# Inverse softmax sums as nine rows or by products, weights summed on TensorE, and a new order of work

## The chip, the cores and the metric

The kernel runs on one core of a Trainium2 chip. The engines of the core work side by side: TensorE (PE, with its weight loads as PEld), VectorE (DVE), ScalarE (ACT), GpSimd (POOL), and SyncE (SP), which issues the DMAs here. Each runs its own instructions in order and waits for the others by semaphores. The metric is the device time of one execution in microseconds. Before the change its median is 1305.22 us over three runs (1303.49 to 1308.19).

## The reference

Attention with a top-32 mask over 8 batches x 8 heads x 576 tokens x 64, then a feed-forward block over the 4608 tokens, all in float32 results:

```python
scores = scale * np.matmul(q, k.transpose(0, 1, 3, 2))
kth = np.partition(scores, -top_k, axis=-1)[..., -top_k:-top_k + 1]
scores = np.where(scores >= kth, scores, -1000000000.0)
scores = scores - np.max(scores, axis=-1, keepdims=True)
attn = np.exp(scores)
attn = attn / (np.sum(attn, axis=-1, keepdims=True) + 1e-09)
attn_out = np.matmul(attn, v)
...
h = x @ w_in                      # x: (4608, 512), w_in: (512, 1024)
e = np.exp(h - h_max)
solu = h * (e / (np.sum(e, axis=-1, keepdims=True) + 1e-09))
ln = (solu - mu) / np.sqrt(var + 1e-06) * g_ln
out = ln @ w_out                  # w_out: (1024, 512)
```

q, k, v arrive as float32. The weights arrive as 64-bit floats (4 MB each), so the kernel has to make float32 out of pairs of 32-bit words itself.

## The kernel before

**Tiling.** The attention part runs in 32 steps, four for each batch. A step takes four chunks of 128 queries (two pairs of heads, two chunks each) and one tile of left-over queries (64 of each of two heads): nine tiles of 128 x 576 scores, which the code numbers j = 0 to 8. Per tile PE makes scores (s_ps, L1951), ACT brings them to SBUF (X, L1960), and ACT and DVE find the 32nd largest score of each row: a first count of entries above an estimated threshold (L1968 on DVE, L1976 on ACT), a second one by signs (sg, L2025), the entries nearest to the threshold (w, L2046), their best eight per half (L2057), and a few merges of small rows (by, L2074 and on). `keep` (L2127, DVE) multiplies the exponentials E by the mask and sums each row into den_all. PE transposes the masked exponentials (tp_p, L2164), ACT copies them out (PT, L2177), and PE multiplies them with v (om, L2220 and L2229).

**The inverse sums.** The product om has head dimensions on its partitions and queries along its free axis, so dividing by the row sums needs the inverse sums spread over partitions. `inverse` (L2133, DVE) takes the reciprocals of 9 columns of 128 sums (rden). `rd_out` (L2138, SP) writes them to a small DRAM buffer, rows, of shape 9 x 128; as the source has queries on partitions, this is a write in 4-byte pieces. `rd_in` (L2145 and L2150, SP) reads the rows back with four DMAs, each broadcast over 64 partitions, into the tile scales (one buffer). `copy_v` (L2243 and L2250, DVE) multiplies om by scales into xTm and xTt, the input of the feed-forward part. A second half of a step has its own copy_v.

**Tokens.** The feed-forward part works on 36 token tiles of 128. `mm1` (h_ps, L2261) multiplies with w_in, `hexp` (ACT, L2272) takes exponentials, `solu` (DVE, L2280) forms the product, `square` (ACT, L2290), `spread` (POOL, L2296 and L2300) and `ln` (POOL, L2303) normalise, `transpose_ln` (PE, L2311) and `copy_ln` (ACT, L2317) turn it, `mm2` (o_ps, L2322) multiplies with w_out, `store` (ACT, L2329) and `send` (SP, L2333) bring it out. Two token tiles of a batch can start once the first two of its four steps are done, the other two after the last two, and one more tile takes the left-over queries of two batches.

**Weights.** There are 16 chunks of 128 x 512 weights, 8 of w_in and 8 of w_out. `load_w` (L1679, SP) brings a chunk of 512 KB as 64-bit words. `w_bits` (DVE, L1696, L1700, L1704) makes a truncated float32 from the high word, and from it the bare power of two. `w_low` (ACT, L1712) turns the low word into a float of at most one unit, `w_mul` (POOL, L1736) multiplies the two, `w_add` (POOL, L1739) adds this correction, and for w_out `w_gain` (POOL, L1746) multiplies by g_ln. The scratch tile w_tmp shares two buffers, the tag solu, with the token part. Near the end the weights are read a second time (w_again) and their exponents checked.

**The order of work.** The instructions of PE, ACT, DVE and POOL are not ordered by hand. `work_of` (L491) lists every operation with its engine, an estimated duration, what it comes after, and which buffers it holds (`room` gives how many there are: 2 of big, tp and o in PSUM, 1 of rb, the scales tile). `arranged` (L734) is a list scheduler over this: it takes, engine by engine, the waiting operation with the lowest rank among those that can start soon. A rank is the step's number times 36000 plus an entry of the table `PLACES` (L812 and on). The whole order is thus fixed when the program is built. SP's DMAs follow in the same order in one queue, so a DMA that waits for data holds those behind it.

At the end of the program `w_verdict` compares counts of checks; were one to fail, a slower general path would compute the output.

Of the kernel before, what the change touches and what calls it, by code (L numbers as in the profile page):

```python
# [15 lines left out]
P = 128  # L16
# [426 lines left out]
class Work:  # L443
# [18 lines left out]
    "ends", "keep", "ln", "key_stats", "w_bits", "w_mul", "w_add", "w_gain",  # L462
# [23 lines left out]

def few_of(i):
    return FEW_COUNTS[i] if i < len(FEW_COUNTS) else FEW


def work_of(B, NP, steps, NF, w_wide):  # L491
# [5 lines left out]
        "xTm": 2, "xTt": 1, "PT0": 1, "PT1": 1, "qkt": 1, "sums": 3, "st": 4, "rb": 1, "rows": 3, "w8": 2, "small": 3,  # L497
# [9 lines left out]
    for b in range(B):  # L507
        for hp in range(NP):
            n = pair(b, hp)
            add(("load_k", n), "SP", 550, behind("load_k", n), [("km", n)], late=2400)  # L510
            add(("load_t", n), "SP", 1650, behind("load_t", n), [("qkt", n)], late=2000)
            add(("load_v", n), "SP", 1650, behind("load_v", n), [("vm", n), (f"vd{n % 4}", n)], late=2400)
            add(("prep_t", n), "PE", 218, [("load_t", n)], [("qkt", n), ("o", ("pre", n)), ("kT", n)], mode="f")
            add(("prep_tc", n), "ACT", 305, [("prep_t", n)], [("o", ("pre", n)), ("kT", n)], 130)
            add(("prep_k", n), "PE", 436, [("load_k", n)], [("km", n), ("tp", ("k", n)), ("kT", n)], mode="f")
# [5 lines left out]
    for i, (b, chunks) in enumerate(steps):  # L521
# [52 lines left out]
        add(("inverse", i), "DVE", 86, [("keep", i, j) for j in range(NT)], [("small", i)], 80)  # L574
        add(("rd_out", i), "SP", 550, [("inverse", i)], [("rows", i), ("small", i)], 2200)
        add(("rd_in", i), "SP", 2200, [("rd_out", i)], [("rows", i), ("rb", i)], 2200)
# [14 lines left out]
        for part in range(2):  # L591
# [18 lines left out]
                [("attn_t", i, part), ("rd_in", i)], [("o", (i, part)), ("rb", i)] + x, 100)  # L610

    def ready_of(n):
        return ("w_gain", n) if n >= 8 else ("w_add", n) if w_wide else ("load_w", n)
# [9 lines left out]
    for m, (b, t, x, made) in enumerate(tokens):  # L623
# [3 lines left out]
        add(("hexp", m), "ACT", 1007, [("mm1", m, 0), ("mm1", m, 1)], [("big", ("h", m)), ("e", m), ("solu", m)], 115)  # L627
# [19 lines left out]
    for n in range(NW):  # L647
        if w_wide:
            tag = ("X", ("w", n)) if 2 <= n < 6 else ("E", ("w", n)) if 6 <= n < 10 else ("lnT", ("w", n))
            add(("load_w", n), "SP", 1700, behind("load_w", n), [tag], 3500)  # L650
            add(("w_bits", n), "DVE", 1600, [("load_w", n)], [tag, ("solu", ("w", n))], 80)
            add(("w_low", n), "ACT", 590, [("w_bits", n)], [tag], 100)
            add(("w_mul", n), "POOL", 1600, [("w_low", n)], [tag, ("solu", ("w", n))])
            add(("w_add", n), "POOL", 1600, [("w_mul", n)], [("solu", ("w", n))])
# [4 lines left out]
        if n >= 8:  # L659
            add(("w_gain", n), "POOL", 1080, [("w_add", n) if w_wide else ("load_w", n), ("copy_g",)])  # L660
# [69 lines left out]
WEIGHT_KINDS = ("load_g", "turn_g", "copy_g", "load_w", "w_bits", "w_low", "w_mul", "w_add", "w_gain")  # L730
# [3 lines left out]
def arranged(work, rank):  # L734
# [23 lines left out]
    while len(start) < len(ops):  # L758
# [56 lines left out]
        "K0": [-269098],  # L815
        "K1": [-754507],
        "K2": [-3281419],
        "K3": [-167927],
        "K4": [-572179],
        "K5": [-504458],  # L820
        "K6": [-165669],
        "K7": [-50556],
        "k0": [-206493],
        "k1": [-596606],
        "k2": [-1347572],
        "k3": [-1214976],
    },
    "load_t": {
        "K0": [-508282],
        "K1": [-149973],  # L830
        "K2": [254494],
        "K3": [79729],
        "K4": [-847916],
        "K5": [124341],
        "K6": [764047],
        "K7": [136089],
        "k0": [-327033],
        "k1": [-94369],
        "k2": [399104],
        "k3": [-638502],  # L840
    },
    "load_v": {
        "K0": [92658],
        "K1": [-145121],
        "K2": [-1256832],
        "K3": [105300],
        "K4": [40735],
        "K5": [-232440],
        "K6": [587722],
        "K7": [168596],  # L850
        "k0": [172383],
        "k1": [-311970],
        "k2": [-126126],
        "k3": [-893372],
    },
    "prep_t": {
        "K0": [-301887],
        "K1": [-1472896],
        "K2": [-2211926],
        "K3": [-87830],  # L860
        "K4": [-605571],
        "K5": [-1210677],
        "K6": [262025],
        "K7": [97718],
        "k0": [-70748],
        "k1": [-1446235],
        "k2": [-655124],
        "k3": [-698217],
    },
    "prep_tc": {  # L870
        "K0": [223057],
        "K1": [-863846],
        "K2": [-877564],
        "K3": [288157],
        "K4": [115939],
        "K5": [-463637],
        "K6": [634678],
        "K7": [292029],
        "k0": [50474],
        "k1": [-597275],  # L880
        "k2": [135481],
        "k3": [-95548],
    },
    "prep_k": {
        "K0": [217554],
        "K1": [423765],
        "K2": [-1151820],
        "K3": [459174],
        "K4": [138923],
        "K5": [239007],  # L890
        "K6": [314486],
        "K7": [542921],
        "k0": [212661],
        "k1": [413375],
        "k2": [429],
        "k3": [407069],
    },
    "prep_kc": {
        "K0": [22479],
        "K1": [-1263182],  # L900
        "K2": [-2452471],
        "K3": [572117],
        "K4": [-155826],
        "K5": [-931816],
        "K6": [48150],
# [1532 lines left out]
```

## Time and profile before

| | us |
|---|---|
| median of three runs | 1305.22 (1303.49 to 1308.19) |
| the profiled execution, its own time | 1310.73 |
| its span, first to last instruction | 1308.9 |
| ACT busy | 1011.4 |
| POOL busy | 209.3 |
| PE busy, mm2 (L2322) | 261.4 in 576 products |
| PE busy, mm1 (L2261) | 263.7 in 576 products |
| DVE busy, best of w (L2057) | 225.8 in 576 instructions |
| DVE busy, keep (L2127) | 236.4 in 288 instructions |
| POOL busy, w_mul and w_add | 46.1 in 32 instructions |

The mean granted TensorE clock is 0.947 of full speed. The DMA engines moved 65.45 MB in 161534 packets; 128136 of these are under 512 bytes.

How to read it: busy time counts the time in which an engine executes something; waits are not in it. In the chain of waits the profile goes back from the last instruction, at each step to what released it, or to the instruction before it on its engine. In a group's row, the idle time is that of the engine just before these instructions, with what ended most of it. In a timeline each row gives the start, the length, engine, line and operation, out<-in, the number merged into the row, and in brackets the idle time ahead of it with its releaser. In the rows of waits the three numbers are the total in us, the times, and the longest.

### The profile page before, as it was taken

How to read it: one execution, taken by the hardware profiler on the slowest of the kernel's cores; microseconds unless marked ns; L12 is line 12 of the kernel's file. 1: busy time of each engine (PE TensorE's matmuls, PEld its weight loads, DVE VectorE, ACT ScalarE, POOL GpSimd, SP SyncE). 2: the span in 40 equal slices, each digit the busy share in tenths (PEclk: the TensorE clock that was granted, in tenths of full speed). 3: DMA queues.
4: the chain of work that ended last, by engine and by line, in shares of the span. 5: the costliest groups of instructions: out<-in, count | busy, mean ns of one | idle time of the engine just before them, and what ended most of it. 6: DMA issues, size and time to landing. Idle time of an engine off the chain costs nothing.

```text
span 1308.9 us, 18612 instructions
## 1 busy us (share of the span) xinstructions
PE 1156.4 (88%) x5731; PEld 658.3 (50%) x5731; DVE 1065.6 (81%) x3065; ACT 1011.4 (77%) x2142; POOL 209.3 (16%) x207
## 2 busy tenths in 40 slices
PE   5660789888999999999999899999999999999977
PEld 3430545455555555555555455555555555555533
DVE  4869749787989889999989589999989689989811
ACT  7773677578897889889796699779796798878732
POOL 3323331010202002020203002020213002110100
PEclk8585899998999999999999899999999999999989
DMA  7231111111131112214130113213120113123630
GB/s 192 79 89 30 43 46 50 36 28 29 20 70 34 31 30 56 73 21 47 47 66 10 30 25 54 70 20 48 43 69 10 30 28 50 38 21 71 150 85 28
DMA packets 161534, 65.45 MB, mean 50 GB/s; under 512 B 128136, under 2 KB 152720, under 8 KB 161424
## 3 DMA queue, kind: packets, MB, share of 16 engines
q1 hardware_dynamic: 161424, 64.15, 22.6%
q8 instruction: 48, 0.79, 0.3%
q14 instruction: 62, 0.51, 0.2%
HBM read 54.53 MB, written 9.58 MB: 49 GB/s over the span
## 4 chain that ended last, share of the span: by engine, by line
DVE 37%; PE 35%; DMA 11%; ACT 11%; issue 3%; SPq 1%; POOL 1%; DVEq 0%; ACTq 0%; POOLq 0%
PE o_ps L2322 8%; DVE E L2127 8%; PE h_ps L2261 8%; DVE w L2046 7%; DVE w L2057 6%; PE s_ps L1951 6%; DMA rows<-rden 6%; DVE junkv L1968 6%; PE om L2220 5%; ACT sg L2025 3%; PE tp_p L2164 3%; ACT X L1960 2%; DVE solu L2280 2%; ACT E L2082 2%; PE tp_ln L2311 1%
## 5 line engine op out<-in xcount | busy, mean ns | idle before, releaser
L2322 PE MATMUL o_ps<-w_out,lnT 128*128 128x512 f32 x576 | 261.4, 599 | 0.3
L2261 PE MATMUL h_ps<-w_in,xTm 128*128 128x512 f32 x512 | 234.8, 605 | 12.7 <-DVE xTm L2243 11.4
L2057 DVE MAX8 w<-w 128x8 f32<-128x288 f32 x576 | 225.8, 445 | 0.5
L2025 ACT ACTIVATE sg<-X,t 128x576 bf16<-128x576 f32 x256 | 197.3, 781 | 29.9 <-DVE t L2010 29.4
L2127 DVE SCALAR_TENSOR_TENSOR E<-X,kth,E 128x576 f32<-128x576 f32 x256 | 210.5, 851 | 4.6 <-ACT E L2082 2.8
L1960 ACT ACTIVATE X<-s_ps 128x576 f32<-128x576 f32 x256 | 163.8, 662 | 62.3 <-PE s_ps L1951 58.2
L2046 DVE SCALAR_TENSOR_TENSOR w<-X,al,sg 128x576 f32<-128x576 f32 x256 | 206.0, 828 | 1.0
L1968 DVE TENSOR_SCALAR_CACHE_REDUCE junkv<-X,t 128x576 bf16<-128x576 f32 x216 | 174.4, 807 | 23.8 <-ACT X L1960 16.3
L2164 PE MATMUL tp_p<-ident,E 128*128 128x128 f32 x1024 | 154.5, 283 | 44.1 <-DVE E L2127 37.5
L1951 PE MATMUL s_ps<-kT,qT 64*128 64x288 f32 x1024 | 177.4, 452 | 3.3 <-ACT X L1960 2.5
L2164 PEld LDWEIGHTS tp_p<-ident,E 128*128 128x128 f32 x1024 | 117.9, 143 | 95.9 <-ACT w_raw L1712 29.1
L2322 PEld LDWEIGHTS o_ps<-w_out,lnT 128*128 128x128 f32 x576 | 106.6, 193 | 110.6 <-issue 108.7
L2177 ACT COPY PT<-tp_p 128x512 f32<-128x512 f32 x256 | 146.9, 595 | 17.4 <-PE tp_p L2164 17.0
L2220 PE MATMUL om<-PT,vm 128*64 128x256 f32 (+1 forms) x1024 | 145.5, 428 | 10.2 <-issue 6.3
L2261 PEld LDWEIGHTS h_ps<-w_in,xTm 128*128 128x128 f32 x512 | 94.4, 193 | 114.0 <-issue 95.9
L2082 ACT ACTIVATE E<-X 128x1152 f32<-128x1152 f32 x128 | 151.0, 1185 | 0.0
L1951 PEld LDWEIGHTS s_ps<-kT,qT 64*128 64x128 f32 x1024 | 99.5, 197 | 67.8 <-issue 30.2
L2296 POOL TENSOR_SCALAR var<-var 128x1 f32<-128x1 f32 x36 | 14.7, 408 | 641.2 <-ACT e_sb L2290 641.2
L1919 POOL TENSOR_TENSOR zs<-zs,phalf 128x9 f32<-128x9 f32 x32 | 61.8, 1934 | 324.2 <-DVE zs L1912 301.7
L2220 PEld LDWEIGHTS om<-PT,vm 128*64 128x64 f32 x1024 | 71.3, 142 | 68.6 <-issue 24.4
L2243 DVE TENSOR_TENSOR xTm<-om,scales 128x256 f32<-128x256 f32 x64 | 26.8, 420 | 69.5 <-DMA scales<-rows 42.8
L2272 ACT ACTIVATE e_sb<-h_ps 128x1024 f32<-128x1024 f32 x36 | 36.8, 1021 | 33.8 <-PE h_ps L2261 33.8
(132 smaller groups left out, 1515.0 us busy)
## 6 DMA issues: line engine op xcount, KB each, us to landing
km<-in_k_dram SPq DMA_DIRECT2D x32, 256.0 KB
q_sb<-in_q_dram SPq DMA_DIRECT2D x128, 64.0 KB
vm<-in_v_dram SPq DMA_DIRECT2D x32, 256.0 KB
scales<-rows SPq DMA_DIRECT2D x64, 128.0 KB
out_dram<-osb SPq DMA_DIRECT2D x32, 256.0 KB
w_raw<-in_moe_w_in_dram SPq DMA_DIRECT2D x8, 512.0 KB
w_raw<-in_moe_w_out_dram SPq DMA_DIRECT2D x8, 512.0 KB
w_again<-in_moe_w_in_dram SPq DMA_DIRECT2D x8, 512.0 KB
```

Of the source, the lines that this page charges most:

```text
L1951: nc.tensor.matmul(out=big[h][:, half, 0:SH], lhsT=queries_of(i, t)[hd, :], rhs=kT[hd, k0 : k0 + SH], start=True, stop=True,)
L1960: nc.scalar.activation(out=x_of(i, j).rearrange("p (a s) -> p a s", a=2), in_=d.pop(("s", j))[:, :, 0:SH], func=AF.Copy, scale=scale,)
L1968: nc.vector.tensor_scalar(out=junk, in0=x_of(i, j), scalar1=st[i][t][:, j : j + 1], scalar2=None, op0=ALU.is_ge, op1=ALU.add, accum_out=co ...
L2025: nc.scalar.activation(out=d["sg", j], in_=x_of(i, j), func=AF.Sign, scale=-(1.0 + 2.0**-23), bias=d["t1"][:, j : j + 1], accum_out=column ...
L2046: nc.vector.scalar_tensor_tensor(out=w, in0=x_of(i, j), scalar=d["al"][:, j : j + 1], in1=d.pop(("sg", j)), op0=ALU.subtract, op1=ALU.mult,)
L2057: nc.vector.max(w8[:, j, 8 * half : 8 * half + 8], w[:, half * SH : (half + 1) * SH])
L2082: nc.scalar.activation(out=d["E", t], in_=d["X", t], func=AF.Exp)
L2127: nc.vector.scalar_tensor_tensor(out=e, in0=x_of(i, j), scalar=d["kth"][:, j : j + 1], in1=e, op0=ALU.is_ge, op1=ALU.mult, accum_out=den_a ...
L2164: nc.tensor.transpose(tp[:, c, :], e[:, c * P : (c + 1) * P], ident)
L2220: nc.tensor.matmul(out=o[h * D : (h + 1) * D, cols], lhsT=vm[:, h, c, :], rhs=pt[:, h * NM + c, :], start=(c == 0), stop=False,)
L2261: nc.tensor.matmul(out=h[:, half, :], lhsT=x[:, c, :], rhs=w_in[:, c, half * 512 : (half + 1) * 512], start=(c == 0), stop=(c == NP - 1),)
L2322: nc.tensor.matmul(out=o, lhsT=d["lnT"][:, c, :], rhs=w_out[:, c, :], start=(c == 0), stop=(c == NF - 1),)
```

## The change

It has three parts.

**Inverse sums.** For steps 0 to 2 (`QUICK`) the DRAM trip is dropped. `spread_r` multiplies each column of inverse sums, broadcast to 64 columns as the stationary operand, with the identity on PE, so that every one of 64 output partitions holds the row; ACT copies it to scales (`copy_s`). For the other 29 steps PE turns the 128 x 9 inverse sums (`turn_r`), ACT copies the 9 x 128 result into the scales tile (`copy_r`), and the write to DRAM is nine rows of 512 bytes; the rows are put in the order head, tile, query, so that the broadcast reads are contiguous. `inverse` becomes two reciprocals for this order.

**Weights.** GpSimd has no part any more. `w_corr` on DVE makes the bare power of two and multiplies it with the low word in one instruction. `w_sum` adds the truncated float32 and the correction in PSUM by two products with the identity, the second in bf16. `w_copy` on ACT copies the sum to its place, times g_ln for w_out. The exponential of token 1 waits for the last `w_sum`.

**Order.** All entries of `PLACES`, the estimates of some DMAs, the patience of the scheduler and its price for a change of PE's mode are new; keys of one pair are prepared after those of the pair before.

```diff
+QUICK = (0, 1, 2)
...
-        add(("rd_out", i), "SP", 550, [("inverse", i)], [("rows", i), ("small", i)], 2200)
-        add(("rd_in", i), "SP", 2200, [("rd_out", i)], [("rows", i), ("rb", i)], 2200)
+        if i in QUICK:
+            for part in range(2):
+                add(("spread_r", i, part), "PE", 436 if part else 654, [("inverse", i)],
+                    [("small", i), ("tp", (i, "r", part))], mode="c")
+                add(("copy_s", i, part), "ACT", 252 if part else 360, [("spread_r", i, part)],
+                    [("tp", (i, "r", part)), ("rb", i)], 140)
+        else:
+            add(("turn_r", i), "PE", 109, [("inverse", i)], [("small", i), ("tp", (i, "r"))], mode="f")
+            add(("copy_r", i), "ACT", 157, [("turn_r", i)], [("tp", (i, "r")), ("rb", i)], 135)
+            add(("rd_out", i), "SP", 550, [("copy_r", i)], [("rows", i), ("rb", i)], 2200)
+            add(("rd_in", i), "SP", 2200, [("rd_out", i)], [("rows", i), ("rb", i)], 3000)
...
+        free = [("w_sum", 15)] if m == 1 and w_wide else []
...
-            add(("w_bits", n), "DVE", 1600, [("load_w", n)], [tag, ("solu", ("w", n))], 80)
-            add(("w_low", n), "ACT", 590, [("w_bits", n)], [tag], 100)
-            add(("w_mul", n), "POOL", 1600, [("w_low", n)], [tag, ("solu", ("w", n))])
-            add(("w_add", n), "POOL", 1600, [("w_mul", n)], [("solu", ("w", n))])
+            add(("w_bits", n), "DVE", 1160, [("load_w", n)], [tag, solu], 80)
+            add(("w_corr", n), "DVE", 1250, [("w_bits", n)], [tag, solu], 80)
+            add(("w_sum", n), "PE", 1290, [("w_corr", n)], [solu, ("tp", ("w", n))], mode="f")
+            add(("w_copy", n), "ACT", 465, [("w_sum", n)] + ([("copy_g",)] if n >= 8 else []), [("tp", ("w", n))], 135)
...
-PATIENCE = {"PE": 82, "ACT": 95, "DVE": 0, "POOL": 3677, "SP": 1016}
-TURNING = 248999
+PATIENCE = {"PE": 171, "ACT": 56, "DVE": 0, "POOL": 18243, "SP": 1014}
+TURNING = 352098
...
+    def w_corr(n):
+
+        val, corr = w_tmp[n][:, 0, :], w_tmp[n][:, 1, :]
         nc.vector.tensor_scalar(
-            out=power, in0=val, scalar1=0xFF800000, scalar2=None, op0=ALU.bitwise_and
-        )
...
+            out=corr.bitcast(U32), in0=val.bitcast(U32), scalar1=0xFF800000, scalar2=None,
+            op0=ALU.bitwise_and,
+        )
+        nc.vector.scalar_tensor_tensor(
+            out=corr, in0=words(n, 0), scalar=2.0**-52, in1=corr, op0=ALU.mult, op1=ALU.mult
+        )
+
+    def w_sum(n):
+
+        tp = w_tmp["sum", n] = ps_tp.tile([P, 512], F32, tag="tp", name="w_tp")
+        nc.tensor.matmul(out=tp, lhsT=ident, rhs=w_tmp[n][:, 0, :], start=True, stop=False)
+        nc.tensor.matmul(
+            out=tp, lhsT=trunc(ident), rhs=trunc(w_tmp[n][:, 1, :]), start=False, stop=True
+        )
+
+    def w_copy(n):
+        dst, _, c = w_chunks[n]
         nc.scalar.activation(
-            out=low_of(n), in_=words(n, 0), func=AF.Copy, scale=2.0**-52
+            out=dst, in_=w_tmp["sum", n], func=AF.Copy,
+            scale=1.0 if c is None else g_col[:, c : c + 1],
         )
...
+    def spread_r(i, part):
...
+        for t in range(2):
+            for h in range(2):
+                j = h * NM + 2 * part + t
+                nc.tensor.matmul(
+                    out=tp[h * D : (h + 1) * D, t * P : (t + 1) * P],
+                    lhsT=d["rden"][:, j : j + 1].broadcast_to([P, D]), rhs=ident,
+                    start=True, stop=True,
+                )
+        if part == 0:
+            for h in range(2):
+                nc.tensor.matmul(
+                    out=tp[h * D : (h + 1) * D, 2 * P : SP],
+                    lhsT=d["rden"][:, 2 * NM : NT].broadcast_to([P, D]),
+                    rhs=ident[:, h * ST : (h + 1) * ST], start=True, stop=True,
+                )
...
+    def turn_r(i):
+        tp = st[i]["tp_r"] = ps_tp.tile([P, NM, P], F32, tag="tp", name="tp_r")
+        nc.tensor.transpose(tp[0:NT, 0, :], st[i]["rden"], ident)
...
     def rd_out(i):
 
         rows = st[i]["rows"] = dram.tile([NT, P], F32, tag="rows", name="rows")
-        nc.sync.dma_start(out=rows.rearrange("j p -> p j"), in_=st[i]["rden"])
+        nc.sync.dma_start(out=rows, in_=st[i]["scales"][0:NT, 0:P])
```

## The prediction

> **What bounds the kernel now.** First the page: busy shares, slices, chain.
>
> ```profile
> PE 1156.4 (88%) x5731; PEld 658.3 (50%) x5731; DVE 1065.6 (81%) x3065; ACT 1011.4 (77%) x2142; POOL 209.3 (16%) x207
> ...
> PE   5660789888999999999999899999999999999977
> ...
> DVE  4869749787989889999989589999989689989811
> ...
> PEclk8585899998999999999999899999999999999989
> ...
> PE o_ps L2322 8%; DVE E L2127 8%; PE h_ps L2261 8%; DVE w L2046 7%; DVE w L2057 6%; PE s_ps L1951 6%; DMA rows<-rden 6%; DVE junkv L1968 6%; PE om L2220 5%; ACT sg L2025 3%; PE tp_p L2164 3%; ACT X L1960 2%; DVE solu L2280 2%; ACT E L2082 2%; PE tp_ln L2311 1%
> ```
>
> Each digit is 32.7 us. The steady stage is PE's; the first seven slices are not: PE has a slice of 0 where DVE has 9. Busy time by stage gives PE idle: 80.5 us of the first 173 (the first h_ps starts at 173.1), 7.4 of 173 to 228, 15.8 of 228 to 330, 34.0 of 330 to 1240, 14.9 of 1240 to 1309. Until token work exists DVE leads, so DVE idle counts at the start, PE idle later. The chain gives 6% to a 4.5 KB write. The same chain in order of time:
>
> ```profile
> 73.35 10.90 DMA rows<-rden
> ...
> 140.67 11.21 DMA rows<-rden
> ...
> 160.87 12.16 DMA rows<-rden
> ...
> 1237.34 12.21 DMA rows<-rden
> 1250.25 5.52 DMA scales<-rows
> ```
>
> Each write takes 9 to 12 us, and SP's queue is in order. Its timeline shows who stands behind, and DVE's waits from 60 to 228 us (total, times, longest) who pays:
>
> ```profile
> 73.35 0.37 SPq L2138 DMA_DIRECT2D rows<-rden  x1
> 84.26 0.62 SPq L2145 DMA_DIRECT2D scales<-rows  x1
> 84.97 0.55 SPq L1679 DMA_DIRECT2D w_raw<-in_moe_w_in_dram  x1
> ```
>
> ```profile
> DVE xTm L2243 <- DMA scales<-rows: 9.1, 2, 5.3
> DVE w_tmp L1696 <- DMA w_raw<-in_moe_w_in_dram: 8.1, 1, 8.1
> ...
> DVE al L2034 <- ACT sg L2025: 7.7, 3, 4.5
> DVE junkv L1968 <- ACT X L1960: 5.7, 2, 3.3
> ...
> DVE w_tmp L1696 <- DMA w_raw<-in_moe_w_out_dram: 2.0, 1, 2.0
> DVE xTt L2250 <- DMA scales<-rows: 1.0, 2, 0.6
> ```
>
> The weight chunk issued at 84.97 waited behind the scales' wait for rows. Last, the end: PE stands 6.41 us for the final scales.
>
> ```profile
> 1256.37 14.58 PE L2261 MATMUL h_ps<-w_in,xTm 128*128 128x512 f32 x28 [6.41 <-DVE xTm L2243]
> ```
>
> **Inverse sums, steps 0 to 2.** Removed: one write and four broadcasts each, with their time on SP. From the inverse to DVE's xTm it took 19.3, 15.2 and 16.1 us (73.1 to 92.4, 140.4 to 155.6, 160.6 to 176.7). Added: a second reciprocal (0.2), ten PE products over 128 columns (four such take 0.60 to 0.66 us, 1.09 at half clock: 1.6 to 2.8 for ten), three ACT copies (0.42 and 0.37 from the PT copies of tp_pt, 0.28 from qTt: 1.0). About 4 us in all. The DVE idle that this removes is 9.1 + 1.0 for scales and 8.1 + 2.0 for chunks held on SP: 20.2 us. The 5.7 us for ACT X goes with it: PE was late there, having waited 4.6 us for an Et keep that stood behind xTm on DVE. I charge 4 us for new waits: copy_v is in order on DVE, and the keeps behind it now wait for ACT's copies.
>
> **Inverse sums, the other 29.** Added: a turn on PE, a copy of 9x128 on ACT (between g_col's 0.16 and qTt's 0.28), then a write of nine 512-byte rows. No row shows that write. Nearest is the 16 KB scales broadcast, 2.6 to 3.4 us from last issue to landing; bounds 2 and 11 (nothing gained), I take 2.7. The broadcasts keep their bytes (128 KB twice, 16 KB twice) and 2.5 us of issue; from first issue to landing 4.6 to 5.5 us, kept at 5. So 0.4 + 0.4 + 0.3 + 2.7 + 5 = 9 us instead of 16.7 (step 3: 227.7 to 244.4), a cut of 7.7.
>
> Here a rule speaks against the change. The Trainium skill, "DMA: Bandwidth & Descriptors", section "Anatomy of one DMA", prices a transfer at about 2.0 us plus bytes over 436 GB/s (fitted on the GpSimd path). At 4.6 KB the old write would take 2.0 us, so these 29 would save nothing and only pay for turns and buffers: +7 us (priced below) in place of their 19.7 saved. The rows above say 9.5 to 12.2 us for the same bytes in 4-byte pieces. I go by the rows.
>
> Where it pays: PE idle behind scales at 242 to 247 (4.98), 286.8 to 288.9 (1.92) and 312.4 to 316.8 (4.39): 11.3 us, each smaller than 7.7, so gone. Between 330 and 1230 DVE waits only 3.2 us for scales; I count 2. At the end the scales land near 1246 instead of 1255.9, but attn_t ends at 1248.1: 6.4 us gone, PE's own om next.
>
> The price: PE is the bound from 330 on. A turn costs between 0.11 (pipelined, from 0.60 for four less 0.17 of tail) and 0.28 us alone; at 0.15, 29 x 0.15 = 4.4 us. It also takes one of two tp buffers, for which PE now waits 0.2 to 0.9 us now and then; between 0 and 0.8 each I take 0.1, 3 us. ACT's 29 x 0.28 = 8 us lies in its 18% of idle. A new wait: the scales buffer is single, and copy_r takes it before the write, where only the broadcasts took it. At 720.4 the write went out at once, but the broadcasts began at 744.85, when the step before had done its last copy_v (744.8). Now write and broadcasts both follow: scales at 754 instead of 750, used at 764.6, so 10 us of slack hide it. A copy_r put too early would hold ACT, with PT copies and evacuations behind it and PE behind those; the bound is nothing to the 24 us of that wait, and as copies are placed by due time I take nothing and leave the rest to the slower rival.
>
> **Weights.** Per chunk POOL loses w_mul and w_add (1.4 each, L1736 and L1739) and, for eight, w_gain (0.8): 52 us of an idle engine. ACT swaps w_low (0.68) for w_copy (0.59, like PT). DVE gains one scalar_tensor_tensor (0.73 pipelined): 16 x 0.73 = +11.7 us on the leading engine. That alone would be a loss, but POOL's work slows DVE:
>
> ```profile
> 32.86 1.40 DVE L1704 TENSOR_SCALAR w_tmp<-w_tmp 128x512 uint32<-128x512 uint32 x1
> ...
> 38.28 0.43 DVE L1704 TENSOR_SCALAR w_tmp<-w_tmp 128x512 uint32<-128x512 uint32 x1
> ```
>
> The first lay beside a w_mul (32.65 to 33.99), the second beside nothing. Seventeen DVE instructions before 185 us are 0.35 to 1.24 us longer beside POOL's weight work, 14.4 us in sum. The Trainium skill, "SBUF — State Buffer", section "Who interferes with whom", has the loser of the shared port pair block for the whole POOL instruction (1.3 to 1.8 us); by it each of the 17 could cost up to 1.3, 22 us; the row's 0.85 mean decides. Net DVE: 14.4 - 11.7 = 2.7 us gained.
>
> PE gains w_sum: one fp32 product of 512 columns (0.43 pipelined, 3.44 for eight) and a bf16 one that no row shows, between 0 and 0.43; I take 0.22. 16 x 0.65 = 10.4 us, 16 at the half clock seen at 20 to 60 us. With the 5 to 8 us of spread_r it lies in the 80 us PE hole; I charge 3 us, and 25 if that cover were gone. The new wait of token 1's exponential for the last w_sum (behind it on ACT: evacuations) binds nothing before: the last chunk was done at 185 us, that exponential near 193.
>
> **The start in sum.** Named waits: 20.2 + 5.7 - 4 + 2.7 = 24.6 us. From above: DVE is idle 63 us of the first 228; less 14.7 in the first 20 us while inputs land and 19 of waits on ACT, PE and early data elsewhere, 29 remain, with the 2.7 some 32. I take 29. No row prices the new order elsewhere: PE's 34 us of idle in the steady stage could vanish or double. Zero, with both ends kept.
>
> Sum: 29 + 11.3 + 2 + 6.4 - 4.4 - 3 - 3 = 38.3 us. Against the profiled execution (1310.73, span 1308.9) that is 1272.4; that execution lies 5.5 above the median, so against 1305.22 it is **1267**.
>
> **Rivals.**
> - *Half of it* (1287): scales arrive early but DVE then waits for ACT's sg or inputs, which already hold it 7.7 + 2.8 us; start 10, middle 6, end 6.4, cost 5. Speaks for it: DVE and ACT are both above 75%. Against: the 8.1 and 9.1 us waits name nothing else.
> - *More* (1240): start 40 and half of the steady idle, 17, since SP no longer stands 11 us a step and PE waits 6.3 us for qk_tails there. Against: few steady waits name SP.
> - *Slower* (1318): the steady order loses. PE is at 96.3% from 330 to 1240, 1.3 us idle a step over some 26 steps. If the added user of tp, copy_r's hold on ACT and the new order cost 2 us more a step, 26 x 2 = 52 us outweigh the start's 38. It decides from 38/26 = 1.5 us a step. For it: PE's waits on PT and lnT copies already exist. Against: they sum to some 12 us in 910.
> - *The edit doing something else*: the slow general path runs only on failed checks of sums and weights, which the diff leaves in place. Under 0.01.
>
> **Chances.** Forecast 0.57, half 0.17, more 0.15, slower 0.09, about no change 0.02. Forecast's own range 1252 to 1282; to leave out 2 in 10, 1240 to 1292. What this kernel's runs can tell from no change is 0.3%. Faster 0.88, same 0.03, slower 0.09.
>
> **What would show it.** rows writes under 4 us and absent for three steps; first h_ps near 145; no w_raw wait behind scales; no 1.4 us tensor_scalar beside weights; the last PE hole gone; steady PE idle near 34 us. Wrong if the first h_ps stays beyond 165, or if eight steps take over 295 us (291.2 now, from the chain's repeat at 480.67, 771.85, 1063.19).

## The result and the profile after

| | before | after |
|---|---|---|
| median | 1306.63 us (4 runs, 1303.49 to 1308.19) | 1246.72 us (4 runs, 1244.19 to 1249.30) |
| after over before, with a 95% interval | | 0.9544 [0.9514, 0.9575] |
| profiled execution, its own time and span | 1310.73, 1308.9 | 1244.19, 1242.4 |
| granted TensorE clock, mean | 0.947 | 0.984 |
| first h_ps | 173.1 | 142.9 |

The change takes 60 us off, where the forecast had 38. The time lies under the forecast's own range (1252 to 1282) and inside the wide one (1240 to 1292). The page of the kernel after, with its busy times, slices and chain by line:

```profile
PE 1158.2 (93%) x5868; PEld 656.7 (53%) x5868; DVE 1059.5 (85%) x3113; ACT 1014.7 (82%) x2180; POOL 144.6 (12%) x167
...
PE   5586899999999999989999999989999999999997
...
DVE  4889999989888988999879888999888888999920
...
PEclk9789999999999999999999999999999999999999
...
PE o_ps L2395 15%; PE h_ps L2334 14%; PE s_ps L1984 9%; PE om L2293 8%; PE tp_p L2237 6%; ACT sg L2058 4%; ACT X L1993 4%; DVE E L2160 3%; DVE w L2090 3%; ACT E L2115 3%; ACT PT L2250 3%; DVE w L2079 3%; DVE junkv L2001 2%; PE om L2302 2%; ACT junka L2009 2%
```

PE's slice of 0 is gone, and it is at 9 from the sixth slice on (31.1 us each) but for two 8s and the last slice; before, it was so only from the eleventh (32.7 us each). Its busy time is the same to 2 us although products were added. The clock row suggests why: its first seven slices are 9789999, and were 8585899 before. The write rows, 6% of the old chain, is in the chain no longer; all DMAs have 0% of it. SP's timeline in step 4 (start, length, instruction) shows it:

```profile
235.72 0.30 SPq L2214 DMA_DIRECT2D rows<-scales  x1
236.99 2.38 SPq L2223 DMA_DIRECT2D scales<-rows  x4
```

The reads of rows go out 1.27 us after the write was issued. Next VectorE's waits between 60 and 228 us, as shown for before (total, times, longest):

```profile
DVE al L2067 <- ACT sg L2058: 4.0, 3, 3.0
DVE junkv L2001 <- ACT X L1993: 3.8, 6, 1.2
DVE stats L1888 <- ACT junka L1877: 0.7, 1, 0.7
DVE E L2160 <- ACT E L2115: 0.6, 1, 0.6
DVE xTm L2316 <- ACT scales L2199: 0.5, 1, 0.5
```

Nothing waits for scales or w_raw from a DMA; what is left are waits for ACT, and they are short. The end, in PE's timeline:

```profile
1189.69 1.24 PE L2302 MATMUL om<-PT,v_diag 128*128 128x320 f32 x4
1190.77 5.74 PE L2334 MATMUL h_ps<-w_in,xTm 128*128 128x512 f32 x13
```

The last h_ps follows om with no bracket, so with no wait; before, PE stood 6.41 us there.

**Where the time went, by stage.** A step's first reciprocal (L2133 before, L2168 after) is a mark that every version has. I cut the span at those of step 4 and step 29, counted from 0:

| us | to step 4 | step 4 to 29 | step 29 to the end | span |
|---|---|---|---|---|
| before | 271.4 | 897.9 | 139.6 | 1308.9 |
| after | 226.0 | 889.1 | 127.4 | 1242.4 |
| gained | 45.4 | 8.9 | 12.2 | 66.5 |

Two cautions. These are single executions: that of before took 4.1 us more than its median, that of after 2.5 less, so 66.5 stands for 59.9 in medians. And a new order moves some work across the marks: between them PE executes 4390 instructions of the old kinds before and 4430 after.

Every experiment is read by the same three stages; they are in one table behind the experiments.

### The profile page after: what moved, and what is told of

It reads as the page before. It is cut to its first block, busy times and chain, and to the rows that moved or that the text cites. A ratio compares the mean times of both kernels' runs of the same rounds, so it can differ in the third digit from the quotient of the medians.

```text
span 1242.4 us, 19028 instructions
## 1 busy us (share of the span) xinstructions
PE 1158.2 (93%) x5868; PEld 656.7 (53%) x5868; DVE 1059.5 (85%) x3113; ACT 1014.7 (82%) x2180; POOL 144.6 (12%) x167
## 4 chain that ended last, share of the span: by engine, by line
PE 59%; ACT 22%; DVE 15%; issue 2%; DMA 0%; POOL 0%; ACTq 0%; DVEq 0%; SPq 0%
PE o_ps L2395 15%; PE h_ps L2334 14%; PE s_ps L1984 9%; PE om L2293 8%; PE tp_p L2237 6%; ACT sg L2058 4%; ACT X L1993 4%; DVE E L2160 3%; DVE w L2090 3%; ACT E L2115 3%; ACT PT L2250 3%; DVE w L2079 3%; DVE junkv L2001 2%; PE om L2302 2%; ACT junka L2009 2%
## 5 line engine op out<-in xcount | busy, mean ns | idle before, releaser
L2395 PE MATMUL o_ps<-w_out,lnT 128*128 128x512 f32 x576 | 257.5, 593 | 0.4 <-DVE xTt L2323 0.2
L2334 PE MATMUL h_ps<-w_in,xTm 128*128 128x512 f32 x512 | 229.3, 593 | 1.6 <-ACT X L1993 1.6
L2160 DVE SCALAR_TENSOR_TENSOR E<-X,kth,E 128x576 f32<-128x576 f32 x256 | 200.5, 814 | 1.8 <-ACT E L2115 0.6
L1984 PE MATMUL s_ps<-kT,qT 64*128 64x288 f32 x1024 | 167.3, 435 | 3.7 <-ACT X L1993 3.7
L2293 PE MATMUL om<-PT,vm 128*64 128x256 f32 (+1 forms) x1024 | 139.0, 417 | 6.6 <-DVE t L1957 3.0
L1984 PEld LDWEIGHTS s_ps<-kT,qT 64*128 64x128 f32 x1024 | 94.1, 189 | 59.6 <-issue 26.1
L2369 POOL TENSOR_SCALAR var<-var 128x1 f32<-128x1 f32 x36 | 11.4, 318 | 608.0 <-ACT e_sb L2363 595.0
L2363 ACT ACTIVATE e_sb<-solu,nmu 128x1024 f32<-128x1024 f32 x36 | 41.3, 1149 | 27.3 <-DVE nmu L2357 23.8
L2067 DVE SCALAR_TENSOR_TENSOR al<-n,tt 128x3 f32<-128x3 f32 x96 | 15.0, 157 | 55.9 <-ACT sg L2058 55.8
```

The source lines that it names most:

```text
L1984: nc.tensor.matmul(out=big[h][:, half, 0:SH], lhsT=queries_of(i, t)[hd, :], rhs=kT[hd, k0 : k0 + SH], start=True, stop=True,)
L2160: nc.vector.scalar_tensor_tensor(out=e, in0=x_of(i, j), scalar=d["kth"][:, j : j + 1], in1=e, op0=ALU.is_ge, op1=ALU.mult, accum_out=den_a ...
L2293: nc.tensor.matmul(out=o[h * D : (h + 1) * D, cols], lhsT=vm[:, h, c, :], rhs=pt[:, h * NM + c, :], start=(c == 0), stop=False,)
L2334: nc.tensor.matmul(out=h[:, half, :], lhsT=x[:, c, :], rhs=w_in[:, c, half * 512 : (half + 1) * 512], start=(c == 0), stop=(c == NP - 1),)
L2395: nc.tensor.matmul(out=o, lhsT=d["lnT"][:, c, :], rhs=w_out[:, c, :], start=(c == 0), stop=(c == NF - 1),)
```

## The experiments

All but three keep the order of the kernel after instruction by instruction and change only what one operation emits, so that the order isn't a second cause. The three are e4, which is about the order, and the two on the last steps. Differences are against 1246.72; kernels were timed in several groups, each with the kernel before beside it, whose median went from 1299.02 to 1306.63. A difference of a few us between groups is therefore near the noise.

**e1: the 4-byte write again, in the 29 steps** (turn and copy stay, without use).

```diff
-        nc.sync.dma_start(out=rows, in_=st[i]["scales"][0:NT, 0:P])
+        nc.sync.dma_start(out=rows.rearrange("j p -> p j"), in_=st[i]["rden"])
```

> The changed kernel in its own order; only the write of the 29 steps goes out in 4-byte pieces again (straight from rden; turn and copy stay, without use). If the length of that write holds back DVE and PE in the middle, at the end and through SP's queue (my account), the write takes 9 to 12 us again and the time rises by 11.3 + 2 + 6.4 less what the free turns leave, and by some waits for query and key tails that land late behind it: 18 to 35 us, so 1265 to 1282. If the writes are hidden anyway and the new order made the gain, it rises by less than 8 us.

1264.68 us, ratio to before 0.9685 [0.9657, 0.9713]: 18.0 over after, at the low edge of the 18 to 35 expected, and not where it was expected: by stages the middle is only 2 us longer (891.1), no more than the scatter, and the end 15.6 longer (143.0). The chain of waits from 1115 us on, DMAs alone (start, length):

```profile
1123.10 9.55 DMA rows<-rden
1134.57 5.62 DMA w_again<-in_moe_w_in_dram
1170.63 11.25 DMA rows<-rden
1183.74 5.31 DMA w_again<-in_moe_w_in_dram
1195.18 13.92 DMA rows<-rden
1210.94 2.48 DMA scales<-rows
```

The writes of the last three steps are in the chain, and between them second readings of weights that stand behind them in SP's queue. From the last inverse to the end it takes 70.9 us instead of 64.6; the other 9.3 us fall between steps 29 and 31.

**e2: the same, and the DRAM trip for steps 0 to 2 too.** Once both halves are spread and copied, the write and the reads follow all the same:

```diff
+        d["spread"] = d.get("spread", 0) + 1
+        if d["spread"] == 2:
+            rd_out(i)
+            rd_in(i)
```

> As the four-byte run, and steps 0 to 2 make the trip through DRAM too (their products and copies stay, without use), so the whole old path of the inverse sums in the new order. My account: the start loses the waits for scales and for chunks held on SP, 20 to 29 us more than the four-byte run. If products for the first steps are worth little because DVE waits for other things there: under 8 us more.

1286.36 us, 0.9856 [0.9829, 0.9883]: 21.7 over the experiment before it, and the profile has 22.9 more by step 4. VectorE's waits up to 228 us in this run, those that matter:

```profile
DVE xTm L2320 <- DMA scales<-rows: 12.3, 2, 11.0
...
DVE w_tmp L1723 <- DMA w_raw<-in_moe_w_in_dram: 7.6, 2, 7.2
...
DVE w_tmp L1723 <- DMA w_raw<-in_moe_w_out_dram: 3.1, 1, 3.1
```

They are the two waits of before, for scales and for the chunks held behind them on SP: 23.0 us, where the forecast had 20.2. Up to step 4, VectorE's busy time (194 us) and its waits for ScalarE (24 us) are the same in e1 and e2, so these waits are the whole difference; the other two terms of the forecast, 5.7 and - 4, don't show.

**e9: the weights as before, with ScalarE and GpSimd instead of VectorE's second instruction and the products.**

```diff
-        nc.vector.scalar_tensor_tensor(
-            out=corr, in0=words(n, 0), scalar=2.0**-52, in1=corr, op0=ALU.mult, op1=ALU.mult
-        )
+        nc.scalar.activation(out=low, in_=words(n, 0), func=AF.Copy, scale=2.0**-52)
+        nc.gpsimd.tensor_tensor(out=power, in0=low, in1=power, op=ALU.mult)
...
+        nc.gpsimd.tensor_tensor(
+            out=w_chunks[n][0], in0=w_tmp[n][:, 0, :], in1=w_tmp[n][:, 1, :], op=ALU.add
+        )
```

> The changed kernel in its own order with the old work on the weights: no products and no copy on PE and ACT for them; ACT's low word, GpSimd's product, sum and gain are back, at the same places. My account: DVE loses one instruction a chunk (11.7 us less) and is held by GpSimd again (some 14 us more), PE is free of 10 us that were hidden: within 6 us of the changed kernel, 1242 to 1253. If the weights on TensorE made the start short: 10 to 25 us slower.

1264.65 us, 0.9697 [0.9671, 0.9723]: 17.9 over after: outside my account (1242 to 1253), inside the other one. The profile has all of it by step 4 (18.0). VectorE is busy 1066.9 us, 7.4 more than after, though it has 16 instructions of 0.695 us fewer: the others took 18.5 us longer. And a new wait stands among PE's, up to 228 us:

```profile
PE tp_ln L2377 <- POOL solu L2369: 7.3, 1, 7.3
```

PE waited for the normalisation of the first tokens. In GpSimd's queue one product of the weights stood between two steps of it, from 169.8 to 172.2 us, so some 2.4 us of this wait are GpSimd's weight work; the rest was late already.

**e10: all old work in the new order** (the edits of e2 and e9 together; the turns, products and copies of the inverse sums stay in it, without use).

> Both old paths in the new order: all the operations of the kernel before, placed by the new ranks. If the operations made the gain: 1285 to 1310, near the kernel before. If the new order alone made most of it: below 1270.

1298.93 us, 0.9950 [0.9930, 0.9971]: 5.2 under the kernel before (1304.09 beside it). By stages: 267.3, 890.2, 140.0. The order thus brings the middle stage from 897.9 to 890.2, although it carries the cost of the unused operations, and leaves start and end about where they were. In the middle, one row of before (PE's waits from 330 to 1250 us) is gone in e10 and in after:

```profile
PE pre L1808 <- DMA qk_tails<-in_q_dram: 6.3, 2, 4.4
```

The 4-byte writes are still in e10, so this wait for query tails went by the order, not by shorter writes.

**e3: GpSimd busy beside the weights**, its results used by nothing:

```diff
+        for _ in range(2):
+            nc.gpsimd.tensor_tensor(out=words(n, 1).bitcast(F32), in0=val, in1=corr, op=ALU.add)
```

> The changed kernel in its own order, with two GpSimd tensor_tensors put beside each weight chunk right after its w_corr (32 in all, results unused). The run with the old weights was 18 us slower than the changed kernel, where my sum had both ways equal. If what GpSimd costs is the time it takes from VectorE beside it (14.4 us by my count of before, more with fuller overlap): 12 to 22 us slower than 1246.7. If it was the longer way through ACT and GpSimd before a weight or a normalised token is ready: under 6 us slower.

1263.81 us, 0.9683 [0.9639, 0.9727]: 17.1 over after. Nobody needs these 32 instructions (1.40 us each by GpSimd's busy time, 189.5 less 144.6), and yet VectorE's busy time grows by 19.0 us, from 1059.5 to 1078.5. VectorE's timeline, and below it GpSimd's in the same stretch:

```profile
32.57 1.16 DVE L2069 SCALAR_TENSOR_TENSOR al<-n,tt 128x3 f32<-128x3 f32 x1 [0.21 <-ACT sg L2060]
33.76 2.64 DVE L2081 SCALAR_TENSOR_TENSOR w<-X,al,sg 128x576 f32<-128x576 f32 x2
...
37.83 1.54 DVE L2081 SCALAR_TENSOR_TENSOR w<-X,al,sg 128x576 f32<-128x576 f32 x2
39.29 0.15 DVE L2069 SCALAR_TENSOR_TENSOR al<-n,tt 128x3 f32<-128x3 f32 x1
```

```profile
32.44 2.61 POOL L1743 TENSOR_TENSOR w_raw<-w_tmp 128x512 f32<-128x512 f32 x2 [2.35 <-DVE w_tmp L1739]
```

While GpSimd runs, from 32.44 to 35.05, the same kind of al takes 1.16 us instead of 0.15, and a pair of w 2.64 instead of 1.54. Up to step 4, VectorE is busy 18.6 us longer than in after and waits 2 us less, while step 4 comes 16.7 later. So it is VectorE's slower instructions that cost the time, and not buffers held longer or GpSimd's late results.

**e11: VectorE's added instruction twice** for each chunk.

```diff
+        nc.vector.scalar_tensor_tensor(
+            out=words(n, 1).bitcast(F32), in0=words(n, 0), scalar=2.0**-52, in1=corr, op0=ALU.mult, op1=ALU.mult
+        )
```

> The changed kernel with VectorE's new scalar_tensor_tensor of each chunk done twice (16 more of 0.69 us; the first result is unused). If VectorE leads until step 4, as my sum has it: 8 to 13 us slower. If it has slack at the start: under 4 us.

1253.58 us, 0.9596 [0.9552, 0.9641]: 6.9 over after, between the two. Sixteen of 0.695 us are 11.1 us, so some 0.62 us of time for each us of VectorE (by the profile's step 4, 8.8 us later, 0.8).

**e12: the products of the weights twice** (both written again into the same buffer).

```diff
+        nc.tensor.matmul(out=tp, lhsT=ident, rhs=w_tmp[n][:, 0, :], start=True, stop=False)
+        nc.tensor.matmul(
+            out=tp, lhsT=trunc(ident), rhs=trunc(w_tmp[n][:, 1, :]), start=False, stop=True
+        )
```

> The changed kernel with the two products of each w_sum done twice (same result). If they lie in PE's idle time at the start, as I charged them with 3 us: 0 to 4 us slower. If they stand in the way of work that VectorE waits for: 8 to 14 us slower.

1259.09 us, 0.9640 [0.9597, 0.9683]: 12.4 over after, as its second expectation had it; the profile has 14.6 by step 4. A second set of products is not hidden: up to the first h_ps PE is idle 44 us in after, where it was 80.5 before, and in e12 VectorE's waits for PE grow from 6.1 to 14.9 us up to step 4, those for ScalarE from 18.9 to 23.5.

**e14: the sum on VectorE instead of the products**, to see whether the first set can be saved:

```diff
-        nc.tensor.matmul(out=tp, lhsT=ident, rhs=w_tmp[n][:, 0, :], start=True, stop=False)
-        nc.tensor.matmul(
-            out=tp, lhsT=trunc(ident), rhs=trunc(w_tmp[n][:, 1, :]), start=False, stop=True
+        nc.vector.tensor_tensor(
+            out=w_chunks[n][0], in0=w_tmp[n][:, 0, :], in1=w_tmp[n][:, 1, :], op=ALU.add
         )
```

> The kernel after, with one edit in the same order: the two parts of a weight chunk are added by one VectorE instruction straight into the weights instead of by products on TensorE, so the products (32 of them in 16 chunks) and the copies out of PSUM of the eight w_in chunks fall away; the w_out chunks still get their gain from ScalarE, in place. Doubling those products cost 12 us, and 11 us more of VectorE there cost 7. Theory (both prices hold in the other direction too): 16 additions of about 0.69 us are 11 us of VectorE, so +7, the products gone -12, some 5 us of ScalarE's copies gone -1 to -3: 3 to 9 us less than the kernel after, about 1238 to 1243 us. Rival (VectorE leads at the start, and TensorE's products cost only when they are doubled): 4 to 8 us more than the kernel after.

1251.06 us, 0.9585 [0.9562, 0.9608]: 4.3 over after, where the rival had 4 to 8. Sixteen additions of 0.68 us are 10.9 us of VectorE; at e11's price that is 6.8, so taking products and eight ScalarE copies away gave back about 2.5. Both figures are near the noise, so all that holds is that the first set of products costs little, and the second 12.

**e4: the new operations with the old order** (the tables of ranks, patience and turning of the kernel before; the new operations keep their new ranks).

```diff
-PATIENCE = {"PE": 171, "ACT": 56, "DVE": 0, "POOL": 18243, "SP": 1014}
-TURNING = 352098
+PATIENCE = {"PE": 82, "ACT": 95, "DVE": 0, "POOL": 3677, "SP": 1016}
+TURNING = 248999
...
```

> All new operations, placed by the ranks, the patience and the mode price of the kernel before (new operations keep their new ranks). The old work in the new order took 5 us less than before. If the order matters as little for the new work: 1247 to 1257. If ranks laid out for the new work are a good part of the gain: 1265 to 1290.

1338.59 us, ratio 1.0240 [1.0191, 1.0288]: 33.7 us slower than before, 91.9 slower than after, and beyond both expectations. Step 4 comes at 221.4, but with less work done by then: between the marks, PE executes 113 more instructions of the old kinds than in after, and this middle takes 965.6. PE's waits from 330 to 1250 us:

```profile
PE tp_p L2229 <- ACT PT L2242: 9.6, 17, 0.9
PE om L2285 <- ACT osb L2394: 8.5, 2, 6.0
PE tp_p L2229 <- ACT lnT L2382: 7.6, 6, 4.5
PE tp_r L2197 <- ACT PT L2242: 4.6, 6, 1.3
```

The first, third and fourth are PE waiting for one of the two tp buffers, which turns now share. They are 4.8, 0 and 2.1 us in after, so they explain a part. In the middle stage PE is idle 57.7 us (39.0 before, 26.2 after) and busy 908 (859 and 863): more than half of the loss is busy time, part of it the work moved in. What else makes it was not settled. It is one order with old ranks, put together by me, not the best that could be found for the new operations.

**e13: four turns instead of one** in each of the 29 steps.

```diff
+        nc.tensor.transpose(tp[0:NT, 1, :], st[i]["rden"], ident)
+        nc.tensor.transpose(tp[0:NT, 2, :], st[i]["rden"], ident)
+        nc.tensor.transpose(tp[0:NT, 3, :], st[i]["rden"], ident)
```

> The kernel after, with one edit in the same order: the turn of the inverse sums in 29 steps is four transposes into the same buffer instead of one (87 more). Theory (a turn is a short product that TensorE must take out of its own time, since PE is busy 93% of the span): each added transpose follows another of its kind and costs about 0.11 to 0.2 us, so the time grows by 10 to 17 us over the kernel after, most of it spread over the steps 3 to 31. Rival (the turns lie in TensorE's idle time, 25 us of it between 330 and 1174 us): it grows by under 4 us. With the first the 4.4 us that the prediction charged for 29 turns stands as a price; with the second it should have been nothing.

1252.77 us: 6.0 over after by medians, between the two expectations. The kernel before ran at 1299.02 beside it, lower than beside the others, and by the ratio to that (0.9658 [0.9628, 0.9688]) the difference would be 15 us. The profile, of the fastest of its four executions as after's is, speaks for the lower: the inverses of step 4 and step 29 come 1.4 and 4.9 us later than after's, the end 5.7. PE's busy time grows by 9.6 us, 0.11 for each of 87 turns; by this profile about half of that, 0.06 us, reaches the time, by the ratio all of it.

**e8b and e8: products on chip for the last step, or the last two** (both put in order anew by the same ranks).

```diff
-QUICK = (0, 1, 2)
+QUICK = (0, 1, 2, 31)
```

> The kernel after with the last step's inverse sums (step 31) going by products on chip as those of steps 0 to 2 do, and with the operations put in order anew by the same ranks. Theory (what is left of the row trip at the end is in the way: after the last inverse 64.6 us pass, and PE is idle 8.5 us of the last 69): 2 to 5 us less than the kernel after. Rival (the trip of 9 rows is already hidden at the end, and the added products and copies take its place): within 2 us of it. Third (the new order disturbs the steps before): 3 us more or worse, which would be seen in the times of the inverses before step 31.

> As the kernel before it, with steps 30 and 31 both going by products on chip. Theory of a trip that is still in the way at the end: 3 to 7 us less than the kernel after. Rival of a hidden trip: within 3 us of it or up to 5 us more, since 12 spreading products and 4 copies are added where PE is busy over 90%.

1252.18 us (0.9636 [0.9617, 0.9655]) with step 31, and 1250.38 us (0.9634 [0.9612, 0.9656]) with 30 and 31 (`QUICK = (0, 1, 2, 30, 31)`). Neither is under after, though the kernel before ran at 1299.02 beside them too: 5.5 and 3.7 over, against the theory of a gain in both. From step 29 to the end they take 130.4 and 130.9 us instead of 127.4. PE's timeline of the second:

```profile
1181.44 0.81 PE L2298 MATMUL om<-PT,v_diag 128*128 128x320 f32 x2
1183.47 1.09 PE L2233 MATMUL tp_p<-ident,E 128*128 128x128 f32 x8 [1.22 <-ACT scales L2197]
...
1193.15 3.17 PE L2330 MATMUL h_ps<-w_in,xTm 128*128 128x512 f32 x7
```

The products and PE's wait for a copy of scales are put where there was no wait to remove; h_ps starts 2.4 us later than in after's lines above. In these two orders the trip of nine rows at the end cost nothing that its removal could save.

**The table of stages**, from one profiled execution each:

| us | median | to step 4 | 4 to 29 | 29 to end |
|---|---|---|---|---|
| before | 1306.63 | 271.4 | 897.9 | 139.6 |
| after | 1246.72 | 226.0 | 889.1 | 127.4 |
| e1 4-byte write | 1264.68 | 231.8 | 891.1 | 143.0 |
| e2 and all trips | 1286.36 | 254.7 | 890.5 | 142.5 |
| e9 old weights | 1264.65 | 244.0 | 890.9 | 127.3 |
| e10 old work, new order | 1298.93 | 267.3 | 890.2 | 140.0 |
| e3 GpSimd beside | 1263.81 | 242.7 | 890.2 | 127.3 |
| e11 VectorE twice | 1253.58 | 234.8 | 889.0 | 127.2 |
| e12 products twice | 1259.09 | 240.6 | 888.8 | 127.6 |
| e14 sum on VectorE | 1251.06 | 233.0 | 890.2 | 127.3 |
| e13 four turns | 1252.77 | 227.3 | 892.6 | 128.2 |
| e8b product in step 31 | 1252.18 | 233.3 | 890.5 | 130.4 |
| e8 in steps 30, 31 | 1250.38 | 224.2 | 890.4 | 130.9 |
| e4 old order | 1338.59 | 221.4 | 965.6 | 150.2 |

The first stage scatters: after, e8 and e8b have the same instructions in the same order up to step 29, and reach step 4 at 226.0, 224.2 and 233.3. A difference under 9 us in that column alone says nothing; there the medians have to speak. The other two columns repeat to about 2 us wherever nothing in them was changed.

## Why the prediction was right in kind and short in size

**What held.** The bound was read rightly: VectorE leads at the start and PE later. The three trips were charged 20.2 + 5.7 - 4, some 22 us, and cost 21.7 (e2 less e1), by the waits that were named. The first h_ps came at 142.9 where 145 was said, the writes are short and absent for three steps, the waits for w_raw, the 1.4 us tensor_scalars and PE's last wait are gone, and eight steps (inverse of step 11 to that of step 19) take 285.8 us instead of 291.2. In the new order the parts are the write 18.0, the three trips 21.7 and the weights 17.9, 57.6 in sum; all three together gave 52.2 (e10 less after). Beside them stands the forecast:

| us | forecast | measured |
|---|---|---|
| three trips | 26.3 (the 29 of the start less VectorE's 2.7) | 21.7 |
| write, 29 steps | 19.7 (11.3 + 2 + 6.4) | 18.0 |
| weights | - 0.3 (2.7 - 3) | 17.9 |
| order, with turns and buffers | - 7.4 (0 - 4.4 - 3) | 5.2 |

The gain that the forecast lacked lies in the last two rows.

**The step that was mis-sized: the weights.** The forecast had + 2.7 for VectorE and - 3 for the products, nothing in all; undoing them costs 17.9. The mark of step 4 is an instruction of VectorE, so the time to it is VectorE's busy time, its waits, and some 4 us of small gaps (us; waits by what ended them):

| to step 4 | busy | for DMA | for ScalarE | for PE | for GpSimd | granted clock |
|---|---|---|---|---|---|---|
| before | 199.0 | 32.5 | 32.5 | 2.5 | 0 | 0.799 |
| after | 193.7 | 0.3 | 18.9 | 6.1 | 2.0 | 0.932 |
| e9 old weights | 200.6 | 0.2 | 29.3 | 5.4 | 4.1 | 0.825 |
| e3 GpSimd beside | 212.3 | 0.4 | 17.5 | 5.4 | 2.2 | 0.902 |
| e8 | 193.6 | 0.2 | 18.9 | 4.5 | 2.0 | 0.931 |
| e8b | 193.8 | 0.7 | 25.4 | 6.6 | 2.0 | 0.898 |

Of e9's 18.0, 6.9 are busy time, the net that the forecast put at 2.7; 10.4 are waits for ScalarE and 2.1 for GpSimd, which it had at nothing. Four terms of it:
- GpSimd's hold on VectorE was put at 14.4 us, from instructions at least 0.35 us longer; e9 shows 18.5 in the new order. e3 shows that such a hold is paid almost in full, 17.1 for 19.0. The Trainium skill, "SBUF — State Buffer", section "Who interferes with whom", has the loser blocked for the whole instruction. The al row agrees (1.0 us lost beside instructions of 1.3 each), while the mean over 32 is 0.59, four tenths of an instruction.
- The 16 x 0.73 us that VectorE gains were charged in full, 11.7. They measure 11.1, and e11 puts the price of as much again at 6.9.
- That GpSimd's queue would give its work sooner was not counted; the forecast saw only 52 us "of an idle engine". It is 2.1 us of VectorE's waits and some 2.4 of PE's wait in e9.
- The waits for ScalarE, the largest, were not counted. With equal work e8b has more of them than e8 at a lower granted clock, and e9 has a lower one still; in e3, where VectorE has more to do, they don't grow at 0.902. How much of the 10.4 is the clock's, and how much the longer way of a weight through ScalarE and GpSimd, stays open.

The products' charge of 3 us is not contradicted (about 2.5 by way of e14 and e11, near the noise), though their size was wrong: 24.4 us of PE busy up to 228 us instead of 10.4. The forecast took one record for one product. One fp32 product is two records, here of 0.59 us each (so the 576 of mm1 and of mm2 in the table of the time before are 288 products each), as this view by tile of the kernel after shows (durations are minimum, median and maximum in ns):

```profile
L1746 PE MATMUL w_tp<-w_tmp,ident x32: 590/594/1222, 12.2 to 166.8; 128*128 128x512 f32 x32
...
L1747 PE MATMUL w_tp<-w_tmp,ident x16: 387/388/634, 14.0 to 167.2; 128*128 128x512 bf16 x16
```

The cover held for one set of them, and e12 shows that it would not have held for twice as much.

**The term that was missing: the granted clock.** The sum priced PE's instructions at the old clock. Busy time by stretch, of before and then of after, from 60 to 120 us (length; PE, PEld, DVE, ACT and POOL busy; granted clock; DMA share; GB/s):

```profile
60.00:120.00 60.00, 23.93 (x140) 14.80 (x140) 48.01 (x116) 39.80 (x92) 17.08 (x12) 0.70 0.25 68
```

```profile
60.00:120.00 60.00, 46.26 (x289) 29.82 (x291) 55.10 (x158) 54.22 (x127) 1.79 (x1) 0.89 0.22 61
```

PE does twice the instructions in the same stretch, at a granted clock of 0.89 instead of 0.70. The Trainium skill, "TensorE: Matmul & The Clock Gate", Part 1, has activity release the throttle, and the two rows go with it. Up to 228 us an s_ps record with qT (L1951, L1984) takes 461 ns on average instead of 551. No edit here changes the clock and nothing else, but two executions do: e8 and e8b, alike in every instruction up to step 29, had 0.931 and 0.898 up to step 4. PE was busy 177.5 and 187.7 us with the same work, VectorE's own work took the same time, it waited 6.5 us longer for ScalarE and 2.1 for PE, and step 4 came 9.1 later. So a lower clock by 0.033 goes with 9 us here. It also shows that the clock is not set by the instructions alone. Before and after differ by 0.133, and in VectorE's waits for ScalarE by 13.6 us, where the forecast had 5.7 less 4; which share of that is the clock's stays open.

**The order.** It was taken as nothing, with both ends kept. With the old work it is worth 5.2 us in medians, the cost of the unused turns and products taken off, and the profile has it in the middle stage, 7.7 of the 8.9 gained there: where PE no longer waits for query tails (6.3 us in the row shown under e10). But it can't be parted from the work: the new operations under old ranks lose 33.7 us (e4), the size that the slower rival feared. Its mechanism, waits at tp, is shown in part only: PE's idle time in that stage is 18.7 us over before's, 0.7 a step, and the rest of the stage's 68 us is busy time. The turns were priced near enough: 0.15 us each in the forecast, between 0.06 (e13, by its profile) and 0.27 (the record of one).

**Middle and end.** The 11.3 us between 228 and 330 were put down to the shorter write. e1 puts the write back, and the middle grows by 2 us at most: PE's waits in e1 between 185 and 340 us name neither scales nor xTm. In the new order the write holds nothing back there, so that gain is not the write's. The end was 6.4 and is 12.2: the last wait was seen (70.9 to 64.6 from the last inverse to the end, as said), but not that w_again stands behind the writes of the steps before. That the write's 19.7 came near the 18.0 of e1 is therefore luck: 13.3 of it were looked for where e1 shows at most 2, and the end, with 6.4, was put at less than half of the 15.6 that e1 shows.

**The rivals.** The time lies closer to "more" (1240) than to the forecast, and in part by its mechanism: the stage to step 4 gained 45 (some 39, if the 6.6 us by which the profiles differ from the medians lie in this stage, the one that scatters), where 29 and the first 5 us of the 11.3 were said, and the rival had 40. But the half of the steady idle that it counted on did not come from SP's writes; it came from the order.

## What to carry to other kernels

Before an engine is called idle and its work free to leave or stay, look at what it does to its neighbours: GpSimd's instructions, wanted by nobody, cost VectorE 0.59 us each and the kernel nearly as much. A write in 4-byte pieces costs what stands behind it in the queue as well as what waits for it, so count both, above all at the start and the end, where nothing covers it. And an order found for one set of operations is part of that set: the same new operations were 60 us faster or 34 us slower than the old kernel, by the order alone. Last, when VectorE waits for ScalarE or PE at a thin start, compare the granted clock before you look for a cause in the program.

## What was not expected of the hardware

- 4.5 KB as nine rows of 512 bytes let the dependent reads go 1.27 us after the issue (1.25 to 3.57 over the 29 steps); in 4-byte pieces the chain of e1 shows 9.6 to 13.9. The Trainium skill's fit in "DMA: Bandwidth & Descriptors", "Anatomy of one DMA", 2.0 us plus bytes and made on the GpSimd path, fits neither of these writes of SP.
- The same instructions in the same order reached step 4 at 224.2 and 233.3 us in two executions (e8, e8b). The latter run's first slices show a granted clock of 8779 (tenths) where the other's show 9799, and VectorE's own work takes the same 194 us in both. Why the clock differed is not known.
- A us more of VectorE cost 0.62 us as an instruction of its own, and 0.90 us as GpSimd's hold (17.1 for 19.0). By the profiles' step 4 it is 0.8 and 0.9, so whether the second weighs more was not settled.
